# Chunked attention and a gated FFN in one kernel: sums and values in two PSUM tiles, memory keys by SyncE, constants laid early, another order in blocks 0 and 1

## The chip, the cores and the metric

The kernel runs on one core of a Trainium2 chip. TensorE (PE in the rows) multiplies matrices and writes to PSUM, ScalarE (ACT) and VectorE (DVE) read and write PSUM and SBUF, GpSimd (POOL) builds masks and issues the DMAs that convert from float32 to float16, and SyncE (SP) issues plain DMAs and DMA transposes. Each engine runs its own list of instructions in order and waits on semaphores. The metric is device microseconds of one execution, lower is better.

## The reference

Attention over chunks of 32 queries, each with 16 tokens of left context, 8 of right context and 8 memory tokens, then a feed-forward network without bias whose gate is a ReLU:

```python
batch, n_heads, seq, head_dim = (4, 8, 768, 64); n_mem = 8
for c in range(seq // 32):
    l_start, r_end = max(0, 32 * c - 16), min(S, 32 * c + 32 + 8)
    k_full = concatenate([mem_k, k[:, :, l_start:r_end]], axis=2)
    v_full = concatenate([mem_v, v[:, :, l_start:r_end]], axis=2)
    a = softmax(q_c @ k_full^T / sqrt(64))
    out[:, :, chunk] = a @ v_full
x = out.transpose(0, 2, 1, 3).reshape(3072, 512)
return (maximum(x @ w_gate, 0) * (x @ w_val)) @ w_out     # 512 -> 1536 -> 512
```

Inputs and output are float32; the kernel computes in float16 with float32 sums.

## The kernel before, in words

The 3072 tokens are cut into eight blocks of 384 (half a sequence). A block has four windows of 96 queries; a window sees 8 memory tokens and a band of up to 120 tokens, so that its scores are one matmul with 128 rows of keys. Heads go in pairs (`hp`, four of them), one head on each half of the partitions.

For a block `n` and a pair `hp` the steps are: `step_s` (in block 0 `step_s0`, which adds the mask by a matmul): the scores on TensorE and their exponential on ScalarE into `ex`; `step_d`: the sums of `ex` over the keys, by four matmuls with a matrix of ones into `xs`; `step_l`: ScalarE's logarithm of `xs`, in place (line 258); `step_e`: ScalarE's exponential of minus that, the reciprocal `rinv` (line 262); `step_v`: the values, eight matmuls into `xo` (line 269); `step_m`: VectorE's product of `xo` and `rinv` into `xT`, the input of the FFN. The tile `X` (`x_ps` in the rows) holds both, `xo` in its first bank of PSUM and `xs` in its second, and there is one such tile.

The FFN of a block is twelve units (`ffn_unit`, eight matmuls each: four with the gate's weights, four with the value's, into one of two PSUM buffers `f_ps`; then ScalarE's ReLU and VectorE's product) and three output units (`out_unit`, twelve matmuls each). Which block's attention step stands behind which unit is written out: by hand for blocks 0 and 1, by `run` for the others. `run` puts the sums, the logarithm and the values of a pair (`d`, `l`, `v`) in a row between the two halves of a unit, two units behind the pair's scores, the exponential behind that unit, and the product ahead of the next one.

Keys and queries of blocks 0 and 1 come as rows and are turned on TensorE (`turn_pe`, then `turn_copy` on VectorE); those of block 2 and later come as bands and are turned by DMA transposes that SyncE issues (`turn_dma`, lines 204 and 206). Half of block 0's rows are staged in float32 (`kst` by SyncE, `qst` by ScalarE's queue) and cast; everything else comes by POOL, in the order of its list, whose numbers are the program's. `fill` issues matmuls on a tile of zeros whose result nobody reads. The framework adds a wait wherever two instructions touch the same tile region in conflicting ways, so far as it can tell them apart.

Of the kernel before, what the change touches and what calls it, by code (L numbers as in the profile page):

```python
# [8 lines left out]
F32 = mybir.dt.float32  # L9
# [8 lines left out]
def kernel(  # L18
# [28 lines left out]
    J = 4  # L47
# [30 lines left out]

    ident = const.tile([128, 128], F16, name="ident")
    sels = [const.tile([128, NQ, 32], F16, name=f"sel{p}") for p in range(2)]  # L80
    kst = const.tile([KR, H // 2, J * D], F32, name="kst")
    qst = const.tile([QR, H // 2, J * D], F32, name="qst")
    k16s = [const.tile([128, NQ, H, D], F16, name=f"k16{p}") for p in range(2)]
    vwins = [const.tile([128, NQ, H, D], F16, name=f"vwin{p}") for p in range(2)]
# [3 lines left out]
    maskk = const.tile([128, 128], F16, name="maskk")  # L88
    maskq = const.tile([128, QB], F16, name="maskq")
    filler = const.tile([128, 512], F16, name="filler")  # L90
    X = xps.tile([128, 2, 512], F32, name="x_ps")
    xo, xs = X[:, 0, 0:TB], X[:, 1, 0:TB]
    mln64 = const.tile([128, 1], F32, name="mln64")
    wg = const.tile([128, NFC, DFF], F16, name="wg")
    wv = const.tile([128, NFC, DFF], F16, name="wv")
# [24 lines left out]
    def load_rows_mem(n):  # L120
        src = bass.AP(tensor=mem_k.tensor, offset=mem_k[n // 2, 0, 0, 0].offset,
                      ap=[[J * D, 2], [NMEM * D, H], [1, J * D]])
        pool_dma(rows_of(n)[0][KR:KR + 2], src)
# [125 lines left out]
    def step_d(n, hp):  # L249
        ex = exs[n, hp]  # L250
        parts = [(0, 1, 1), (1, NQ, 0)] if n % 2 == 0 else [(0, NQ - 1, 0), (NQ - 1, NQ, 2)]
        for i0, i1, kind in parts:
            for hh in range(2):
                nc.tensor.matmul(xs[D * hh:D * hh + D, QB * i0:QB * i1], lhsT=ones[:, kind, :],  # L254
                                 rhs=ex[:, hh, i0:i1, :], start=True, stop=True)

    def step_l(n, hp):
        nc.scalar.activation(xs, xs, ACT.Ln, scale=1.0 / 64.0)  # L258

    def step_e(n, hp):  # L260
        rinv = rpool.tile([128, TB], F32, name="rinv")
        nc.scalar.activation(rinv, xs, ACT.Exp, scale=-1.0, bias=mln64)  # L262
        rinvs[n, hp] = rinv
# [58 lines left out]
            out_unit(n, u - NDC, between)  # L322


    def fill(count, cols=512):
        ps = fps.tile([128, 2, 512], F32, tag="f", name="idle")
        for i in range(count):
            nc.tensor.matmul(ps[:, 0, 0:cols], lhsT=filler[:, 0:128], rhs=filler[:, 0:cols], start=True, stop=True)


    nc.scalar.preload_act_table_set("natural_log_exp_and_others")
    for hp in range(HP // 2):
        sp(kst[:, 2 * hp:2 * hp + 2], k_rows(0, 2 * hp, 2))
        act_dma(qst[:, 2 * hp:2 * hp + 2], q_rows(0, 2 * hp, 2))
    load_rows_mem(0)
    fetch_mem(memv, mem_v)

    def words(t):
        return t.bitcast(U32)

    zero(filler, 0.0)
    zero(words(ident), 0)
    zero(words(sels[0].rearrange("p i t -> p (i t)")), 0)


    zero(words(maskk), 0)
    zero(words(maskq), 0)
# [11 lines left out]
    zero(ones[96:128, 2], 0.0)  # L359
    zero(ones[96:120, 2], 1.0)  # L360
    zero(mln64, -LN64)
    zero(words(vwins[0][0:NMEM + 16, 0].rearrange("p h d -> p (h d)")), 0)
    zero(words(vwins[1][96:128, NQ - 1].rearrange("p h d -> p (h d)")), 0)

    def select(ap, fill_with, base, pattern, mult, op=ALU.not_equal):
        nc.gpsimd.affine_select(out=ap, in_=ap, compare_op=op, fill=fill_with, base=base, pattern=pattern,
# [10 lines left out]

    select(ident, 1.0, 0, [[-1, 128]], 1)
    build_sel(0)
    load_rows(0, 4, 4)  # L380
    loads_v(0)
    load_w(0, 256)
    load_w(256, 512)

    def cast(t, hp, eng):
        dst, src = rows_of(0)[t], (kst, qst)[t]
        eng(dst[0:(KR, QR)[t], 2 * hp:2 * hp + 2], src[:, 2 * hp:2 * hp + 2])

    fill(9)
    cast(0, 0, dve_copy)  # L390
    cast(1, 0, act_copy)
    turn_pe(0, 0)
    turn_copy(0, 0)
    fill(3)
    cast(0, 1, act_copy)
    cast(1, 1, act_copy)
    step_s0(0, 0)
    turn_pe(0, 1)
    turn_copy(0, 1)
    fill(1)  # L400
# [12 lines left out]
    step_v(0, 0)
    step_m(0, 0)
    step_s0(0, 3)
    step_d(0, 2)
    step_l(0, 2)
    step_e(0, 2)


    zero(words(sels[1].rearrange("p i t -> p (i t)")), 0)
    build_sel(1)
    zero(bias, 0.0)
    zero(words(k16s[0][0:32, 0].rearrange("p h d -> p (h d)")), 0)
    zero(words(k16s[1][96:128, NQ - 1].rearrange("p h d -> p (h d)")), 0)
    load_w(512, 1024)
    load_rows_mem(1)
    load_rows(1, 0, 4)
    load_rows(1, 4, 4)

    select(bias, NEG, -NMEM, [[-32, 3]], 1, ALU.is_ge)
    select(bias, 0.0, -NMEM, [[0, 3]], 1, ALU.is_ge)
    select(bias, NEG, NMEM + 55, [[32, 3]], -1, ALU.is_ge)
    load_w(1024, 1280)
    loads_v(1)
    load_w(1280, 1536)
# [44 lines left out]
    step_s(1, 2)
    step_d(1, 0)
    step_l(1, 0)
    step_e(1, 0)
    step_v(1, 0)
    step_m(1, 0)
    ffn_unit(0, 9)
    step_s(1, 3)
    step_d(1, 1)
    step_l(1, 1)  # L490
    step_e(1, 1)
    step_v(1, 1)
    step_m(1, 1)
    ffn_unit(0, 10)
    step_d(1, 2)
    step_l(1, 2)
    step_e(1, 2)
    step_v(1, 2)
    step_m(1, 2)
    ffn_unit(0, 11)  # L500
    step_d(1, 3)
    step_l(1, 3)
    step_e(1, 3)
    step_v(1, 3)
    step_m(1, 3)
# [68 lines left out]
```

## Time and profile before

| | before |
|---|---|
| median of 3 runs | 275.13 us (273.32 to 278.44) |
| the profiled execution | 276.26 us, span 274.6 us |
| mean granted clock of TensorE | 0.975 |
| TensorE busy | 242.1 us, 88% of the span |
| ScalarE busy | 128.5 us, 47% |
| VectorE busy | 81.1 us, 30% |
| POOL busy | 87.7 us, 32% |

The span runs from the first to the last instruction of the profiled execution; the time around it is 1.7 us. A busy share is an average over the whole span, which has stages with different limits. The granted clock is the share of TensorE's full clock that was granted: 1.00 is 2.4 GHz and 0.50 is 1.2 GHz; values between are stretches with both.

### The profile page before, as it was taken

Reading aid. Unit: us, or ns where it says so; the run is one execution under the profiler, and the core shown is the slowest. Engines: PE = TensorE matmul, PEld = TensorE weight load, DVE = VectorE, ACT = ScalarE, POOL = GpSimd, SP = SyncE. Lnnn points to the kernel's source line nnn. Section 1 sums busy time; section 2 is a strip of 40 time slices with the busy share of each in tenths; the row PEclk is TensorE's granted clock in tenths of the full one; section 3 lists DMA queues with packets and bytes.
Section 4 is the critical chain, followed back from the end, with each engine's and each line's share of the span. In section 5 each row is a group of like instructions: output and inputs, shape, how many; then the busy total and the mean of one; then the engine's idle time right before and its main releaser. Section 6 shows DMA issues by size and latency. Waiting matters only on the chain.

```text
span 274.6 us, 4565 instructions
## 1 busy us (share of the span) xinstructions
PE 242.1 (88%) x1845; PEld 128.9 (47%) x1845; DVE 81.1 (30%) x161; ACT 128.5 (47%) x276; POOL 87.7 (32%) x116
## 2 busy tenths in 40 slices
PE   5957983889998999999899999899999998999994
PEld 1633562445444455544454455444554454545541
DVE  3533472223033124321334033311342033313420
ACT  4442347232475256634565266534664365623421
POOL 8757789236901930077003910050000000000000
PEclk9988999669999999999999999999999999999999
DMA  7999999999993998199931996094600200011002
GB/s 153 162 138 198 180 166 181 172 145 157 174 180 91 133 183 117 24 58 187 144 72 11 153 160 134 2 94 111 127 0 2 115 0 4 0 76 41 0 29 85
DMA packets 113780, 28.56 MB, mean 104 GB/s; under 512 B 100224, under 2 KB 110688, under 8 KB 113760
## 3 DMA queue, kind: packets, MB, share of 16 engines
q0 software_dynamic: 86960, 15.17, 69.0%
q1 hardware_dynamic: 26384, 12.72, 19.8%
q10 hardware_dynamic: 416, 0.39, 0.5%
q8 instruction: 14, 0.23, 0.4%
q14 instruction: 6, 0.05, 0.1%
HBM read 31.15 MB, written 6.29 MB: 136 GB/s over the span
## 4 chain that ended last, share of the span: by engine, by line
PE 85%; ACT 9%; DMA 2%; issue 1%; DVE 1%; DVEq 0%; ACTq 0%; POOLq 0%
PE f_ps L286 49%; PE o_ps L311 23%; ACT x_ps L258 5%; PE x_ps L269 4%; PE x_ps L254 3%; PE sc_ps L218 3%; DMA rk<-in_mem_k_dram 2%; ACT rinv L262 1%; ACT ex L240 1%; PE kq_ps L185 1%; PE kq_ps L190 1%; ACT gr L292 1%; DVE gv L293 0%; DVE kq L199 0%; PE sc_ps L226 0%
## 5 line engine op out<-in xcount | busy, mean ns | idle before, releaser
L293 DVE TENSOR_TENSOR gv<-f_ps,gr 128x384 f16<-128x384 f32 x96 | 53.4, 557 | 151.6 <-ACT gr L292 151.6
L286 PE MATMUL f_ps<-xT,wg 128*128 128x384 f16 x384 | 81.5, 333 | 0.8 <-DVE gv L293 0.8
L286 PE MATMUL f_ps<-xT,wv 128*128 128x384 f16 x384 | 81.6, 333 | 0.0
L292 ACT ACTIVATE gr<-f_ps 128x384 f16<-128x384 f32 x96 | 47.0, 491 | 71.4 <-PE f_ps L286 69.4
L311 PE MATMUL o_ps<-wo,gv 128*128 128x512 f16 x288 | 63.8, 379 | 0.0
L136 POOL DMA_DIRECT2D vwin<-in_v_dram x32 | 28.8, 910 | 75.0 <-PE x_ps L269 72.2
L286 PEld LDWEIGHTS <-wg 128*128 128x128 f16 x384 | 35.6, 99 | 26.5 <-issue 2.4
L286 PEld LDWEIGHTS <-wv 128*128 128x128 f16 x384 | 36.2, 99 | 24.4 <-issue 1.9
L311 PEld LDWEIGHTS <-gv 128*128 128x128 f16 x288 | 28.0, 98 | 32.8
L314 ACT COPY o_sb<-o_ps 128x512 f32<-128x512 f32 x24 | 14.0, 585 | 45.2 <-PE o_ps L311 45.2
L240 ACT ACTIVATE ex<-sc_ps,bias 128x256 f16<-128x256 f32 x84 | 33.5, 477 | 2.5 <-PE sc_ps L218 2.5
L269 PE MATMUL x_ps<-ex,vwin 128*64 128x96 f16 x256 | 12.1, 215 | 24.3 <-ACT x_ps L258 13.6
L269 PEld LDWEIGHTS <-vwin 128*64 128x64 f16 x256 | 11.0, 113 | 29.4 <-issue 29.0
L273 DVE TENSOR_TENSOR xT<-x_ps,rinv 128x384 f16<-128x384 f32 x32 | 17.8, 555 | 23.3 <-PE x_ps L269 13.8
L136 POOL DMA_DIRECT2D k<-in_k_dram x24 | 21.5, 911 | 6.5 <-DMA wo<-in_moe_w_out_dram 5.5
L258 ACT ACTIVATE x_ps<-x_ps 128x384 f32<-128x384 f32 x32 | 15.3, 478 | 15.6 <-PE x_ps L254 15.5
L157 POOL DMA_DIRECT2D q16n<-in_q_dram x24 | 18.7, 807 | 6.2 <-DMA vwin<-in_v_dram 4.9
L262 ACT ACTIVATE rinv<-x_ps,mln 128x384 f32<-128x384 f32 x32 | 18.4, 576 | 0.2
L254 PE MATMUL x_ps<-ex,ones 128*64 128x96 f16 (+1 forms) x128 | 11.7, 264 | 0.0
L199 DVE CAST kq<-kq_ps 128x896 f16<-128x896 f32 x8 | 8.7, 1090 | 5.8 <-PE kq_ps L190 5.8
L254 PEld LDWEIGHTS <-ones 128*64 128x64 f16 x128 | 4.8, 110 | 10.1 <-issue 9.9
L218 PEld LDWEIGHTS <-kT 64*128 64x128 f16 x192 | 4.8, 94 | 7.8 <-issue 7.8
(51 smaller groups left out, 67.6 us busy)
## 6 DMA issues: line engine op xcount, KB each, us to landing
out_dram<-o_sb SPq DMA_DIRECT2D x24, 256.0 KB, 2.3
vwin<-in_v_dram POOLq DMA_DIRECT2D x24, 120.0 KB, 4.9
q16n<-in_q_dram POOLq DMA_DIRECT2D x24, 96.0 KB, 6.4
k<-in_k_dram POOLq DMA_DIRECT2D x18, 120.0 KB, 6.3
wo<-in_moe_w_out_dram POOLq DMA_DIRECT2D x3, 512.0 KB, 9.7
wg<-in_moe_w_gate_dram POOLq DMA_DIRECT2D x4, 256.0 KB, 7.8
wv<-in_moe_w_val_dram POOLq DMA_DIRECT2D x4, 256.0 KB, 8.0
rk<-in_k_dram POOLq DMA_DIRECT2D x3, 224.0 KB, 7.4
```

The costliest lines, as they stand in the source:

```text
L136: pool_dma(dsts[p][NMEM + m0:NMEM + m1, i], src)
L157: pool_dma(q16s[n][:, i], src)
L240: nc.scalar.activation(ex[:, :, :, s], src, ACT.Exp, scale=SCALE, bias=bias[:, g:g + 1])
L254: nc.tensor.matmul(xs[D * hh:D * hh + D, QB * i0:QB * i1], lhsT=ones[:, kind, :], rhs=ex[:, hh, i0:i1, :], start=True, stop=True)
L258: nc.scalar.activation(xs, xs, ACT.Ln, scale=1.0 / 64.0)
L262: nc.scalar.activation(rinv, xs, ACT.Exp, scale=-1.0, bias=mln64)
L269: nc.tensor.matmul(xo[D * hh:D * hh + D, QB * i:QB * i + QB], lhsT=vw[:, i, 2 * hp + hh, :], rhs=ex[:, hh, i, :], start=True, stop=True)
L273: nc.vector.tensor_tensor(out=x_of(n)[:, hp, :], in0=xo, in1=rinvs.pop((n, hp)), op=ALU.mult)
L286: nc.tensor.matmul(ps[:, a, 0:TB], lhsT=(wg, wv)[a][:, f, 128 * m:128 * m + 128], rhs=xTs[n][:, f, :], start=(f == 0), stop=(f == NFC - 1))
L292: nc.scalar.activation(gr, ps[:, 0, 0:TB], ACT.Relu)
L293: nc.vector.tensor_tensor(out=gvs[n][:, m, :], in0=ps[:, 1, 0:TB], in1=gr, op=ALU.mult)
L311: nc.tensor.matmul(o_ps, lhsT=gvs[n][:, m, 128 * t:128 * t + 128], rhs=wo[:, m, :], start=(m == 0), stop=(m == NDC - 1))
```

## The change

Sums and values get two tiles of one bank each, so that `xo` and `xs` are tiles of their own. The memory keys of heads 0 to 3 of block 0 go by SyncE, between its two loads of staged keys, into two further rows of `kst`, and are cast with them; both casts of keys are now on VectorE and both of queries on ScalarE. POOL loads the rows of heads 4 to 7 first. The memsets of `sel1`, `bias` and the window of block 0's values stand ahead of the attention of block 0; those of the other windows come after it. The weights are loaded in the order 0, 256, 512 (256 columns each), then block 1's rows, then 768, block 1's values, and 1024 to 1536 in one piece. The fillers are 18 matmuls of 384 columns into `xo` instead of 13 of 512 into a buffer of the FFN. In block 0 the order of turns, scores and sums is another; in block 1 the turns stand two units earlier, and the sums of a pair stand a unit ahead of its values.

```diff
-    kst = const.tile([KR, H // 2, J * D], F32, name="kst")
+    kst = const.tile([KR + 2, H // 2, J * D], F32, name="kst")
...
-    X = xps.tile([128, 2, 512], F32, name="x_ps")
-    xo, xs = X[:, 0, 0:TB], X[:, 1, 0:TB]
+    xo, xs = (xps.tile([128, 512], F32, name=nm)[:, 0:TB] for nm in ("xo_ps", "xs_ps"))
...
-        sp(kst[:, 2 * hp:2 * hp + 2], k_rows(0, 2 * hp, 2))
+        sp(kst[0:KR, 2 * hp:2 * hp + 2], k_rows(0, 2 * hp, 2))
         act_dma(qst[:, 2 * hp:2 * hp + 2], q_rows(0, 2 * hp, 2))
-    load_rows_mem(0)
-    fetch_mem(memv, mem_v)
+        if hp == 0:
+            load_rows_mem(sp, kst[KR:KR + 2], 0, 0, H // 2)
+    load_rows(0, 4, 4)
+    load_rows_mem(pool_dma, rows_of(0)[0][KR:KR + 2, H // 2:H], 0, H // 2, H // 2)
...
+    zero(words(sels[1].rearrange("p i t -> p (i t)")), 0)
+    zero(bias, 0.0)
...
-    load_rows(0, 4, 4)
+    fetch_mem(memv, mem_v)
     loads_v(0)
-    load_w(0, 256)
-    load_w(256, 512)
+    for c0 in (0, 256, 512):
+        load_w(c0, c0 + 256)
...
-    fill(9)
-    cast(0, 0, dve_copy)
-    cast(1, 0, act_copy)
-    turn_pe(0, 0)
-    turn_copy(0, 0)
-    fill(3)
-    cast(0, 1, act_copy)
-    cast(1, 1, act_copy)
+    fill(11)
+    for hp in range(2):
+        cast(0, hp, dve_copy)
+        cast(1, hp, act_copy)
+        turn_pe(0, hp)
+        turn_copy(0, hp)
+    fill(4)
     step_s0(0, 0)
...
-    load_w(512, 1024)
-    load_rows_mem(1)
+    load_rows_mem(pool_dma, rows_of(1)[0][KR:KR + 2], 1, 0, H)
     load_rows(1, 0, 4)
     load_rows(1, 4, 4)
...
-    load_w(1024, 1280)
+    load_w(768, 1024)
+    zero(words(vwins[1][96:128, NQ - 1].rearrange("p h d -> p (h d)")), 0)
     loads_v(1)
-    load_w(1280, 1536)
+    load_w(1024, 1536)
...
-    for m in range(2, 8):
+    for m in range(2, 6):
         ffn_unit(0, m)
     turn_pe(1, 0)
     turn_copy(1, 0)
...
+    ffn_unit(0, 6)
+    sums(1, 0)
+    step_s(1, 2)
+    ffn_unit(0, 7)
+    sums(1, 1)
+    step_s(1, 3)
+    values(1, 0)
     ffn_unit(0, 8)
```

Here `sums` is `d`, `l`, `e` of a pair and `values` is `v`, `m`.

TensorE in block 3, where the second pair's sums and values stand between the halves of a unit (`ones` are the sums, `vwin` the values; the numbers in brackets name the semaphore of the engine that is waited for). Before:

```order
L254 MATMUL x_ps<-ex,ones 64x288 [waits Activation_49]
L254 LDWEIGHTS ones
L254 MATMUL x_ps<-ex,ones 64x288
L254 LDWEIGHTS ones
L254 MATMUL x_ps<-ex,ones 64x96
L254 LDWEIGHTS ones
L254 MATMUL x_ps<-ex,ones 64x96
L269 LDWEIGHTS vwin_101
L269 MATMUL x_ps<-ex,vwin_101 64x96 [waits Activation_49]
```

And now:

```order
L253 MATMUL xs_ps<-ex,ones 64x288 [waits Activation_49]
L253 LDWEIGHTS ones
L253 MATMUL xs_ps<-ex,ones 64x288
L253 LDWEIGHTS ones
L253 MATMUL xs_ps<-ex,ones 64x96
L253 LDWEIGHTS ones
L253 MATMUL xs_ps<-ex,ones 64x96
L268 LDWEIGHTS vwin_101
L268 MATMUL xo_ps<-ex,vwin_101 64x96
```

Nothing moved here; the first matmul of the values no longer names ScalarE's semaphore.

POOL at the start of the program, from the end of block 0's values on (`sel_95` is block 1's selection matrix, `rk` and `rq` block 1's rows). Before:

```order
L170 DMA wv<-in_moe_w_val_dram 128x4x256
L366 AFFINE_SELECT sel_95<-sel_95 128x4x28
L366 AFFINE_SELECT sel_95<-sel_95 128x3x2
L366 AFFINE_SELECT sel_95<-sel_95 128x4x2
L170 DMA wg<-in_moe_w_gate_dram 128x4x512
L170 DMA wv<-in_moe_w_val_dram 128x4x512
L123 DMA rk<-in_mem_k_dram 2x8x256
```

And now:

```order
L169 DMA wg<-in_moe_w_gate_dram 128x4x256
L169 DMA wv<-in_moe_w_val_dram 128x4x256
L368 AFFINE_SELECT sel_95<-sel_95 128x4x28
L368 AFFINE_SELECT sel_95<-sel_95 128x3x2
L368 AFFINE_SELECT sel_95<-sel_95 128x4x2
L122 DMA rk<-in_mem_k_dram 2x8x256
```

The weights from column 512 on moved ahead of the selects, cut to 256 columns, and block 1's rows follow the selects at once; the other 256 columns come behind those rows.

ScalarE in block 1, where the attention stands between the units of block 0 (`gr` is the ReLU of a unit). Before, with the first pair's logarithm and exponential:

```order
L240 ACTIVATE ex<-sc_ps,bias 128x8x32 x6
L292 ACTIVATE gr<-f_ps 128x384
L240 ACTIVATE ex<-sc_ps,bias 128x8x32 x3
L258 ACTIVATE x_ps<-x_ps 128x384
L262 ACTIVATE rinv<-x_ps,mln_110 128x384
```

And now:

```order
L239 ACTIVATE ex<-sc_ps,bias 128x8x32 x6
L291 ACTIVATE gr<-f_ps 128x384
L257 ACTIVATE xs_ps<-xs_ps 128x384
L261 ACTIVATE rinv<-xs_ps,mln_111 128x384
L239 ACTIVATE ex<-sc_ps,bias 128x8x32 x3
```

The first pair's logarithm and exponential moved ahead of the third pair's three score exponentials.

## Rows read from the trace of the kernel before

**Rows 1.** the page's part 4: the chain that ended last, by line

```profile
PE f_ps L286 49%; PE o_ps L311 23%; ACT x_ps L258 5%; PE x_ps L269 4%; PE x_ps L254 3%; PE sc_ps L218 3%; DMA rk<-in_mem_k_dram 2%; ACT rinv L262 1%; ACT ex L240 1%; PE kq_ps L185 1%; PE kq_ps L190 1%; ACT gr L292 1%; DVE gv L293 0%; DVE kq L199 0%; PE sc_ps L226 0%
```

**Rows 2.** waits: engine, line, waited for: us in total, times, longest

```profile
PE x_ps L269 <- ACT x_ps L258: 13.6, 24, 0.6
PE x_ps L269 <- ACT rinv L262: 10.7, 7, 2.1
```

**Rows 3.** timeline of TensorE, one pair: start, us, [idle before <-releaser]

```profile
99.25 0.81 PE L286 MATMUL f_ps<-xT,wg 128*128 128x384 f16 x4
99.99 0.36 PE L254 MATMUL x_ps<-ex,ones 128*64 128x288 f16 x4
100.92 0.36 PE L269 MATMUL x_ps<-ex,vwin 128*64 128x96 f16 x8 [0.57 <-ACT x_ps L258]
101.21 0.82 PE L286 MATMUL f_ps<-xT,wv 128*128 128x384 f16 x4
```

**Rows 4.** timeline of TensorE, block 0: sums and what follows

```profile
10.38 0.36 PE L254 MATMUL x_ps<-ex,ones 128*64 128x96 f16 x4
10.57 0.60 PE L185 MATMUL kq_ps<-sel,rk 114*64 114x128 f16 x8
```

**Rows 5.** windows: us; busy us PE, PEld, DVE, ACT, POOL; clock, DMA share, GB/s

```profile
119.00:149.00 30.00, 27.73 (x213) 14.55 (x211) 8.57 (x16) 15.67 (x35) 10.07 (x13) 1.00 0.96 106
```

**Rows 6.** DMA issues around 1.2 to 2.1: KB each, us to landing

```profile
kst<-in_k_dram SPq DMA_DIRECT2D x2, 224.0 KB, 3.6
rk<-in_mem_k_dram POOLq DMA_DIRECT2D x1, 8.0 KB, 5.2
```

**Rows 7.** timeline of VectorE: the first copy of a turn

```profile
7.74 1.09 DVE L199 CAST kq<-kq_ps 128x896 f16<-128x896 f32 x1 [2.85 <-PE kq_ps L190]
```

**Rows 8.** timeline of TensorE, 0 to 72: four starts with their waits

```profile
6.75 0.63 PE L185 MATMUL kq_ps<-sel,rk 114*64 114x128 f16 x8 [1.52 <-DMA rk<-in_mem_k_dram]
43.56 0.36 PE L269 MATMUL x_ps<-ex,vwin 128*64 128x96 f16 x8 [2.10 <-ACT rinv L262]
56.44 0.53 PE L269 MATMUL x_ps<-ex,vwin 128*64 128x96 f16 x8 [1.19 <-ACT rinv L262]
68.80 0.34 PE L218 MATMUL sc_ps<-qT,kT 64*128 64x96 f16 x8
```

**Rows 9.** windows, columns as in 5: two stretches with a low granted clock

```profile
18.75:22.95 4.20, 3.70 (x27) 1.39 (x21) 1.11 (x2) 0.46 (x1) 4.06 (x9) 0.60 1.10 156
49.71:59.33 9.62, 7.25 (x41) 3.62 (x41) 2.23 (x4) 3.05 (x6) 2.53 (x3) 0.50 1.54 159
```

**Rows 10.** timeline of POOL: block 1's selects

```profile
16.73 0.62 POOL L366 TENSOR_SCALAR_AFFINE_SELECT sel<-sel 128x112 f16<-128x112 f16 x3 [4.95 <-DVE bias L423]
```

**Rows 11.** windows of 1 us: the last two numbers are DMA share and GB/s

```profile
18.00:19.00 1.00, 0.48 (x9) 0.35 (x9) 0.00 (x0) 0.47 (x1) 1.00 (x3) 0.85 0.46 23
19.00:20.00 1.00, 1.00 (x4) 0.30 (x2) 0.56 (x1) 0.00 (x0) 1.00 (x2) 0.50 0.66 59
20.00:21.00 1.00, 1.00 (x11) 0.48 (x11) 0.19 (x1) 0.00 (x0) 1.00 (x3) 0.50 1.20 197
```

**Rows 12.** timeline of SyncE's queue: staged keys, block 2's transposes

```profile
0.81 0.90 SPq L333 DMA_DIRECT2D kst<-in_k_dram  x2
44.39 7.42 SPq L204 DMA_TRANSPOSE kT<-k  x1
51.99 4.74 SPq L206 DMA_TRANSPOSE qT<-q16n  x1
```

**Rows 13.** DMA issues at 44.39, 51.99, and 76.9 to 82.5: transposes, us to landing

```profile
kT<-k SPq DMA_TRANSPOSE x1, 14.2
...
qT<-q16n SPq DMA_TRANSPOSE x1, 11.3
...
kT<-k SPq DMA_TRANSPOSE x1, 6.9
qT<-q16n SPq DMA_TRANSPOSE x1, 3.7
```

More of the change, by code (lines that the diff above doesn't have):

```diff
@@ L118, in rows_of, with load_rows_mem @@
         return rows[n]
[L120 to L123, printed above, removed]
+    def load_rows_mem(dma, dst, n, h0, nh):
+        src = bass.AP(tensor=mem_k.tensor, offset=mem_k[n // 2, h0, 0, 0].offset,
+                      ap=[[J * D, 2], [NMEM * D, nh], [1, J * D]])
+        dma(dst, src)
     def load_rows(n, h0, nh):
@@ L322, in unit, with fill @@
             out_unit(n, u - NDC, between)
-    def fill(count, cols=512):
-        ps = fps.tile([128, 2, 512], F32, tag="f", name="idle")
+    def fill(count, cols=TB):
         for i in range(count):
-            nc.tensor.matmul(ps[:, 0, 0:cols], lhsT=filler[:, 0:128], rhs=filler[:, 0:cols], start=True, stop=True)
+            nc.tensor.matmul(xo[:, 0:cols], lhsT=filler[:, 0:128], rhs=filler[:, 0:cols], start=True, stop=True)
     nc.scalar.preload_act_table_set("natural_log_exp_and_others")
     for hp in range(HP // 2):
-        sp(kst[:, 2 * hp:2 * hp + 2], k_rows(0, 2 * hp, 2))
+        sp(kst[0:KR, 2 * hp:2 * hp + 2], k_rows(0, 2 * hp, 2))
         act_dma(qst[:, 2 * hp:2 * hp + 2], q_rows(0, 2 * hp, 2))
-    load_rows_mem(0)
-    fetch_mem(memv, mem_v)
+        if hp == 0:
+            load_rows_mem(sp, kst[KR:KR + 2], 0, 0, H // 2)
+    load_rows(0, 4, 4)
+    load_rows_mem(pool_dma, rows_of(0)[0][KR:KR + 2, H // 2:H], 0, H // 2, H // 2)
     def words(t):
         return t.bitcast(U32)
-    zero(filler, 0.0)
     zero(words(ident), 0)
     zero(words(sels[0].rearrange("p i t -> p (i t)")), 0)
+    zero(words(filler), 0)
+    zero(words(vwins[0][0:NMEM + 16, 0].rearrange("p h d -> p (h d)")), 0)
     zero(words(maskk), 0)
@@ L361 @@
     zero(mln64, -LN64)
-    zero(words(vwins[0][0:NMEM + 16, 0].rearrange("p h d -> p (h d)")), 0)
-    zero(words(vwins[1][96:128, NQ - 1].rearrange("p h d -> p (h d)")), 0)
+    zero(words(sels[1].rearrange("p i t -> p (i t)")), 0)
+    zero(bias, 0.0)
     def select(ap, fill_with, base, pattern, mult, op=ALU.not_equal):
@@ L379 @@
     build_sel(0)
-    load_rows(0, 4, 4)
+    fetch_mem(memv, mem_v)
     loads_v(0)
-    load_w(0, 256)
-    load_w(256, 512)
+    for c0 in (0, 256, 512):
+        load_w(c0, c0 + 256)
     def cast(t, hp, eng):
-        dst, src = rows_of(0)[t], (kst, qst)[t]
-        eng(dst[0:(KR, QR)[t], 2 * hp:2 * hp + 2], src[:, 2 * hp:2 * hp + 2])
-    fill(9)
-    cast(0, 0, dve_copy)
-    cast(1, 0, act_copy)
-    turn_pe(0, 0)
-    turn_copy(0, 0)
-    fill(3)
-    cast(0, 1, act_copy)
-    cast(1, 1, act_copy)
+        dst, src, n = rows_of(0)[t], (kst, qst)[t], (KR + 2, QR)[t]
+        eng(dst[0:n, 2 * hp:2 * hp + 2], src[:, 2 * hp:2 * hp + 2])
+    fill(11)
[5 more added lines that the diff above has]
+    fill(4)
     step_s0(0, 0)
-    turn_pe(0, 1)
-    turn_copy(0, 1)
-    fill(1)
+    turn_pe(0, 2)
+    turn_copy(0, 2)
     step_d(0, 0)
     step_l(0, 0)
+    step_s0(0, 1)
     step_e(0, 0)
-    turn_pe(0, 2)
-    step_s0(0, 1)
-    turn_copy(0, 2)
     turn_pe(0, 3)
+    turn_copy(0, 3)
+    fill(1)
+    step_s0(0, 2)
     step_d(0, 1)
     step_l(0, 1)
-    step_s0(0, 2)
-    turn_copy(0, 3)
     step_e(0, 1)
+    fill(2)
+    step_s0(0, 3)
     step_v(0, 0)
     step_m(0, 0)
-    step_s0(0, 3)
     step_d(0, 2)
@@ L418 @@
     step_e(0, 2)
-    zero(words(sels[1].rearrange("p i t -> p (i t)")), 0)
     build_sel(1)
-    zero(bias, 0.0)
-    zero(words(k16s[0][0:32, 0].rearrange("p h d -> p (h d)")), 0)
-    zero(words(k16s[1][96:128, NQ - 1].rearrange("p h d -> p (h d)")), 0)
-    load_w(512, 1024)
-    load_rows_mem(1)
+    load_rows_mem(pool_dma, rows_of(1)[0][KR:KR + 2], 1, 0, H)
     load_rows(1, 0, 4)
@@ L433 @@
     select(bias, NEG, NMEM + 55, [[32, 3]], -1, ALU.is_ge)
-    load_w(1024, 1280)
+    load_w(768, 1024)
+    zero(words(vwins[1][96:128, NQ - 1].rearrange("p h d -> p (h d)")), 0)
     loads_v(1)
-    load_w(1280, 1536)
+    load_w(1024, 1536)
+    zero(words(k16s[0][0:32, 0].rearrange("p h d -> p (h d)")), 0)
+    zero(words(k16s[1][96:128, NQ - 1].rearrange("p h d -> p (h d)")), 0)
     fetch_mem(memk, mem_k)
@@ L454 @@
     chunk(0, 0)
+    step_d(0, 3)
+    step_l(0, 3)
+    step_e(0, 3)
     step_v(0, 2)
@@ L457 @@
     chunk(0, 1)
-    step_d(0, 3)
-    step_l(0, 3)
-    step_e(0, 3)
     step_v(0, 3)
@@ L466, with sums, values @@
     loads_v(2)
-    for m in range(2, 8):
+    def sums(n, hp):
+        step_d(n, hp)
+        step_l(n, hp)
+        step_e(n, hp)
+    def values(n, hp):
+        step_v(n, hp)
+        step_m(n, hp)
+    for m in range(2, 6):
         ffn_unit(0, m)
@@ L479 @@
     turn_copy(1, 3)
-    ffn_unit(0, 8)
[L481 to L486, printed above, removed]
-    ffn_unit(0, 9)
[L488 to L493, printed above, removed]
-    ffn_unit(0, 10)
[L495 to L499, printed above, removed]
-    ffn_unit(0, 11)
[L501 to L505, printed above, removed]
+    ffn_unit(0, 6)
[5 more added lines that the diff above has]
+    values(1, 0)
+    ffn_unit(0, 8)
+    values(1, 1)
+    sums(1, 2)
+    ffn_unit(0, 9)
+    values(1, 2)
+    sums(1, 3)
+    ffn_unit(0, 10)
+    values(1, 3)
+    ffn_unit(0, 11)
     STEP = {"s": step_s, "d": step_d, "l": step_l, "e": step_e, "v": step_v, "m": step_m}
```

## The prediction

> **What bounds the kernel now.** I read the chain that ended last first, by line: TensorE's FFN and output matmuls hold 72% of it, but ScalarE's logarithm, line 258, is third with 5% [rows 1]. A function that should run beside TensorE has no business there. The list of waits says whom it holds up: the value matmuls of line 269 waited 24 times for line 258, 13.6 us in all, and 7 times for the exponential of line 262, 10.7 us [rows 2]. The first turn, at 6.75, waited 1.52 us for the memory keys [rows 8]. 24 is six blocks times four head pairs, so the first wait is the steady part, and the timeline shows one: sums at 99.99, values only at 100.92, with 0.57 us idle between, though the values read nothing that the logarithm writes [rows 3]. The seven others lie in blocks 0 and 1, ahead of the first scores of block 2 at 68.80 [rows 8]. So I cost two stretches apart: from 68.80 to the end, where TensorE alone sets the pace, and from 0 to 68.80, where transfers may.
>
> **The steady part: two tiles.** The sums and the values of a pair lay in one PSUM tile, so each value group waited for line 258 to have done with that tile. In the changed program no first value matmul waits for ScalarE any more; some wait for VectorE's multiplication of the pair before, one to three units earlier. What is saved for a pair is 0.93 us from the start of the sums to the start of the values [rows 3], less what the sums take when something follows at once. That is bounded by 0.19 us (sums at 10.38, next group at 10.57 [rows 4]) and by 0.29 us, the time of the value group, which has as many columns and twice the weight loads [rows 3]. That leaves 0.64 to 0.74; the idle time alone would give 0.57. I take 0.65, near the lower end, since weights change shape there: 24 x 0.65 = **15.6 us** (13.7 to 17.8). What is late next? ScalarE has 15.67 us of work in 30 us, VectorE 8.57 [rows 5]; with TensorE some 2.6 us faster per block ScalarE stands at 57%, and the logarithm now runs under the values and the second half of the unit, so I add nothing.
>
> **The start.** The keys of memory for heads 0 to 3 now go by SyncE into the staging tile. They took 5.2 us from POOL's issue, the staged keys 3.6 us from SyncE's [rows 6]. SyncE starts at 0.81 and needs 0.45 us an issue [rows 12]; issued second they land near 0.81 + 0.45 + 3.6 = 4.9. With half a microsecond for the cast, now of 114 rows, the first turn starts at 5.4 for 6.75: 1.3 us earlier. The second half of the staged keys is issued one place later, about 0.45 us, which nobody waits for: its cast stands behind a copy of 1.09 us on VectorE [rows 7]. That queueing is the price of taking the cast from ScalarE: the second turn comes about 1 us later than it might. The fillers are 18 x 384 columns for 13 x 512, 4% more, into the values' tile, which is free then: nothing.
>
> **Blocks 0 and 1.** In block 1 the sums of a pair are now issued a unit ahead of its values, so that the logarithm and the exponential run under an FFN unit (twice four matmuls of 0.7 us [rows 3]). Its four waits, two of 2.10 (43.56) and two of 1.19 (56.44) [rows 8], 6.6 us, go. Of the other 4.1 us of the seven waits, in block 0, I take 3, since there two of the waits are replaced by waits for the same ScalarE queue. With the waits went the clock: the granted clock was 0.60 over 18.75 to 22.95 and 0.50 (1.2 GHz of the two levels) over 49.71 to 59.33, the second time soon after the two waits of 2.10 us. TensorE was busy 3.70 and 7.25 us there [rows 9]; at 2.4 GHz these would be 2.2 and 3.6, so 1.5 + 3.6 = 5.1 are to be had. If only TensorE counted, the scores of block 2 would come 1.3 - 1.0 + 3 + 6.6 + 5.1 = 15.0 us earlier, at 53.8.
>
> **But the transfers do not move by 15 us.** Those scores need the transposes of block 2's keys and queries, which SyncE issued at 44.39 and 51.99 [rows 12] and which landed 14.2 and 11.3 us later [rows 13], at 58.6 and 63.3: 5.5 us ahead of their use at 68.80. They follow the loads of block 2, which are at the end of POOL's list, behind all weights, keys and values of blocks 0 and 1, and the changed list carries the same bytes ahead of them. The engines that move them were busy all the while but for one hole: POOL waited 4.95 us for a memset [rows 10], and the rate fell to 23 and 59 GB/s in two microseconds beside 197 [rows 11]. The constants laid early take this wait away: (2 x 197 - 82) / 197 = 1.6 us. Block 0's rows now ahead of POOL's selects fill up to another 1 us between 5 and 9, where POOL's issue was the limit; I take 0.5. So the queries land at 63.3 - 2.1 = 61.2 and the scores move by **7.6 us** (5.5 if the loads do not move at all, 15.0 if the transposes cease to matter). TensorE stands idle for the rest, 61.2 - 53.8 = 7.4 us, at the first scores of block 2. Splitting weights 512 to 1023 in two and joining 1024 to 1535 moves no bytes; unit 8 may wait up to 1 us for the joined load, inside those 7.4.
>
> What the skill says to this: the Trainium skill, DMA: Bandwidth & Descriptors (Issuing engines are not separate DMA queues), has all issuers run on the same 16 engines, so that issuing elsewhere saves the issue time alone. The rates of rows 11 agree; taken strictly it would give the move to SyncE nothing beyond its 1.3 us, which the idle time swallows.
>
> **After that idle time the clock is low.** The two stretches of rows 9 cost 1.5 and 3.6 us, the second behind idle times of 2.10 us. A 7 us gap is longer, but the output unit behind it is dense, like the units that ended both; I take **2 us** (0 to 3.6). The Trainium skill, TensorE: Matmul & The Clock Gate (HAM oscillation), describes the same: a wait for data sends the array to half its clock, and the next work starts cold. No stretch of this trace has a gap of that length, so only the direction is borne out.
>
> **The sum**, against the profiled execution's 276.26 us: 15.6 + 7.6 - 2.0 = 21.2, so 255.1. That execution lies 0.4% above the median of 275.13; from the median, 253.9: I say **254**.
>
> **Rivals.**
> 1. The transposes do not hold TensorE. For it: later transposes landed in 6.9 and 3.7 us, half and a third of 14.2 and 11.3 [rows 13]; if block 2's meet a shorter queue to that degree, the queries are there by about 51.99 - 2.1 + 3.7 = 53.6. Against: the weights of the output, the next values and keys are queued beside them as before. Then 275.1 - 15.6 - 15.0 = 244.5. Chance 0.20.
> 2. The first part gives nothing: the loads come no earlier, and the cold stretch after the wait eats the 5.5 us of slack. Against it: rows 11 show a hole that a memset made. Then 275.1 - 13.7 = 261.4. Chance 0.10.
> 3. The wait in the steady part stays under another name: the values then wait for VectorE's multiplication, or the next unit for ScalarE. Against: that multiplication is issued a unit or more ahead, and ScalarE has 43% to spare. Only the first part is left: 275.1 - 5.6 = 269.5. Chance 0.05.
> 4. Slower: the clock stays at 1.2 GHz after TensorE's wait for the transposes, because block 2's scores, sums and values interrupt the units of that stretch. Every microsecond of work there costs a second one. It decides from 23 us of such work, and is worth 281 from 29 us. Against: the longest such stretch had 3.6 us of work (7.25 at half), and in all steady blocks, with a wait in every third unit, the clock was 1.00 [rows 5]. Chance 0.02.
>
> **How the numbers follow.** Forecast 0.60 (249 to 260: 17.8 + 7.6 at one end, 13.7 + 5.5 - 3.6 at the other), rivals 0.20, 0.10, 0.05, 0.02, other things 0.03. The range 244 to 261 holds the forecast's case, most of the first rival's and some of the second's: 0.8. About 2% is what can be told from no change; 269.6 is that bound. Faster 0.95, within 2% 0.03, slower 0.02.
>
> **What the changed profile would show.** Right: no wait of the values for the logarithm; each steady block 2.6 us shorter from its first scores to the next block's; the four waits of block 1 gone; the last wait of TensorE ahead of block 2's first scores 4 to 8 us long, put down to a transfer; clock 0.5 for a few microseconds behind it and 1.00 ahead of it. The prediction is wrong if those scores come before 57 or after 65, if steady blocks keep a wait above 0.2 us, or if the low clock behind the transposes lasts longer than 8 us.

## The result and the profile after

| | before | after |
|---|---|---|
| median | 275.72 us (4 runs, 273.32 to 278.44) | 251.79 us (4 runs, 251.0 to 254.03) |
| the profiled execution | 276.26 us, span 274.6 | 251.0 us, span 249.3 |
| mean granted clock | 0.975 | 0.983 |
| TensorE busy | 242.1 us, 88% | 235.5 us, 94% |

The ratio is 0.917, with a 95% interval of 0.908 to 0.927. The forecast of 254 us and its range hold the time. Here and below medians are over all runs, while ratios leave out executions more than 1.5% above the fastest of the same kernel.

The chain by line, which had line 258 in third place [rows 1]:

```profile
PE f_ps L285 43%; PE o_ps L310 25%; DMA wv<-in_moe_w_val_dram 8%; DMA qT<-q16n 4%; DMA wo<-in_moe_w_out_dram 3%; PE xs_ps L253 3%; PE sc_ps L217 3%; POOL vwin L135 3%; PE xo_ps L268 2%; SPq L203 1%; POOL wg L169 1%; POOL wv L169 1%; POOL q16n L156 1%; POOL rk L126 0%; POOL memv L138 0%
```

No line of ScalarE is left. In its place stand loads: weights, the queries' transpose and POOL's issues. The chain leaves TensorE and goes back through loads, so that one wait for data decides what lies ahead of it. The list of TensorE's waits names it in its first line, and neither line of [rows 2] has a successor:

```profile
PE sc_ps L217 <- DMA qT<-q16n: 4.0, 1, 4.0
PE kq_ps L184 <- DVE rk L389: 1.7, 1, 1.7
...
PE xo_ps L268 <- DVE xT L272: 0.7, 2, 0.4
```

A steady pair in TensorE's timeline, beside [rows 3]: the values start 0.19 us behind the sums, where 0.93 us lay between, and nothing is idle.

```profile
89.92 0.36 PE L253 MATMUL xs_ps<-ex,ones 128*64 128x288 f16 x4
90.11 0.34 PE L268 MATMUL xo_ps<-ex,vwin 128*64 128x96 f16 x8
90.38 0.82 PE L285 MATMUL f_ps<-xT,wv 128*128 128x384 f16 x4
```

That is 0.74 us a pair, 24 x 0.74 = 17.8 us. The first 67 us in the same view: the first two turns, the first output unit, and the first scores of block 2, which [rows 8] had at 68.80 with no wait.

```profile
5.21 0.74 PE L184 MATMUL kq_ps<-sel,rk 114*64 114x128 f16 x8
...
7.96 0.63 PE L184 MATMUL kq_ps<-sel,rk 114*64 114x128 f16 x8 [1.68 <-DVE rk L389]
...
53.42 2.75 PE L310 MATMUL o_ps<-wo,gv 128*128 128x512 f16 x12
60.20 0.51 PE L217 MATMUL sc_ps<-qT,kT 64*128 64x96 f16 x8 [4.03 <-DMA qT<-q16n]
60.64 5.46 PE L310 MATMUL o_ps<-wo,gv 128*128 128x512 f16 x18
66.03 0.36 PE L253 MATMUL xs_ps<-ex,ones 128*64 128x96 f16 x4
```

Windows, with the columns of [rows 5]; the third number from the end is the granted clock. It is low in two stretches, one behind the wait of 1.68 us and one behind that of 4.03 us; the two of [rows 9] are gone.

```profile
9.00:12.40 3.40, 3.40 (x28) 1.99 (x28) 1.05 (x1) 0.81 (x1) 3.40 (x6) 0.51 1.92 154
...
60.00:61.00 1.00, 0.80 (x9) 0.46 (x10) 0.00 (x0) 0.26 (x1) 0.66 (x2) 0.55 2.13 181
61.00:62.00 1.00, 1.00 (x4) 0.41 (x3) 0.00 (x0) 0.94 (x3) 0.48 (x1) 0.50 1.64 260
62.00:63.00 1.00, 1.00 (x4) 0.35 (x3) 0.00 (x0) 0.00 (x0) 0.22 (x1) 0.50 2.22 176
63.00:64.00 1.00, 1.00 (x5) 0.35 (x4) 0.00 (x0) 0.00 (x0) 1.00 (x2) 0.74 2.41 153
```

SyncE's queue issued block 2's transposes 2.4 and 3.0 us earlier than in [rows 12], and the keys' landed 13.2 us later (14.2 in [rows 13]):

```profile
42.04 6.74 SPq L203 DMA_TRANSPOSE kT<-k  x1
48.97 4.56 SPq L205 DMA_TRANSPOSE qT<-q16n  x1
```

So of the 25.3 us between the two profiled executions, 8.6 came ahead of the first scores of block 2 (68.80 to 60.20). The stretch behind them fell from 205.8 to 189.1 us, by 16.7, which is the pairs' 17.8 less the low clock.

### The profile page after: what moved, and what is told of

It reads as the page before. It is cut to its first block, busy times and chain, and to the rows that moved or that the text cites. A ratio compares the mean times of both kernels' runs of the same rounds, so it can differ in the third digit from the quotient of the medians.

```text
span 249.3 us, 4594 instructions
## 1 busy us (share of the span) xinstructions
PE 235.5 (94%) x1850; PEld 127.1 (51%) x1850; DVE 81.3 (33%) x162; ACT 127.6 (51%) x275; POOL 87.4 (35%) x116
## 4 chain that ended last, share of the span: by engine, by line
PE 74%; DMA 15%; POOL 6%; issue 2%; SPq 1%; ACT 0%; POOLq 0%
PE f_ps L285 43%; PE o_ps L310 25%; DMA wv<-in_moe_w_val_dram 8%; DMA qT<-q16n 4%; DMA wo<-in_moe_w_out_dram 3%; PE xs_ps L253 3%; PE sc_ps L217 3%; POOL vwin L135 3%; PE xo_ps L268 2%; SPq L203 1%; POOL wg L169 1%; POOL wv L169 1%; POOL q16n L156 1%; POOL rk L126 0%; POOL memv L138 0%
## 5 line engine op out<-in xcount | busy, mean ns | idle before, releaser
L285 PE MATMUL f_ps<-xT,wg 128*128 128x384 f16 x384 | 79.4, 327 | 0.8 <-DVE gv L292 0.8
L285 PE MATMUL f_ps<-xT,wv 128*128 128x384 f16 x384 | 79.3, 327 | 0.0
L310 PE MATMUL o_ps<-wo,gv 128*128 128x512 f16 x288 | 65.2, 385 | 0.0
L272 DVE TENSOR_TENSOR xT<-xo_ps,rinv 128x384 f16<-128x384 f32 x32 | 17.7, 553 | 17.3 <-ACT rinv L261 14.4
L257 ACT ACTIVATE xs_ps<-xs_ps 128x384 f32<-128x384 f32 x32 | 15.3, 479 | 11.8 <-PE xs_ps L253 10.2
L261 ACT ACTIVATE rinv<-xs_ps,mln 128x384 f32<-128x384 f32 x32 | 18.4, 576 | 0.2
L217 PE MATMUL sc_ps<-qT,kT 64*128 64x96 f16 x192 | 8.4, 208 | 4.0 <-DMA qT<-q16n 4.0
L268 PE MATMUL xo_ps<-ex,vwin 128*64 128x96 f16 x256 | 11.0, 207 | 0.7 <-DVE xT L272 0.7
L253 PE MATMUL xs_ps<-ex,ones 128*64 128x96 f16 (+1 forms) x128 | 11.4, 258 | 0.0
L268 PEld LDWEIGHTS <-vwin 128*64 128x64 f16 x256 | 8.7, 110 | 2.8 <-issue 2.4
```

Of the source, the lines that this page charges most:

```text
L217: nc.tensor.matmul(sc[:, hh, QB * i:QB * i + QB], lhsT=kT[s, i, hp, :], rhs=qT[s, i, hp, :], start=start, stop=start or i == NQ - 1)
L268: nc.tensor.matmul(xo[D * hh:D * hh + D, QB * i:QB * i + QB], lhsT=vw[:, i, 2 * hp + hh, :], rhs=ex[:, hh, i, :], start=True, stop=True)
L272: nc.vector.tensor_tensor(out=x_of(n)[:, hp, :], in0=xo, in1=rinvs.pop((n, hp)), op=ALU.mult)
L285: nc.tensor.matmul(ps[:, a, 0:TB], lhsT=(wg, wv)[a][:, f, 128 * m:128 * m + 128], rhs=xTs[n][:, f, :], start=(f == 0), stop=(f == NFC - 1))
L310: nc.tensor.matmul(o_ps, lhsT=gvs[n][:, m, 128 * t:128 * t + 128], rhs=wo[:, m, :], start=(m == 0), stop=(m == NDC - 1))
```

## The experiments

The theory is the prediction's: two tiles give the steady part, and in the first 60 us the transposes hold what the other edits free. The rivals were that the edits other than the tiles carry the first part, or that the transposes do not matter. Unless said otherwise an edit is made to the changed kernel.

**The two tiles alone**, in the kernel before:

```diff
-    X = xps.tile([128, 2, 512], F32, name="x_ps")
-    xo, xs = X[:, 0, 0:TB], X[:, 1, 0:TB]
+    xo, xs = (xps.tile([128, 512], F32, name=nm)[:, 0:TB] for nm in ("xo_ps", "xs_ps"))
```

> The kernel before with the two tiles alone. Theory (the shared tile costs 0.74 us a pair in the steady part, and the first scores of block 2 cannot start before their queries are turned): 24 x 0.74 = 17.8 less behind those scores; in blocks 0 and 1 the values no longer wait for ScalarE either, so TensorE comes to the scores early and waits there for the queries at about 63.3 instead of 68.8, 5.5 less, and some 1.6 us are lost to the low clock behind that wait: 275.7 - 17.8 - 5.5 + 1.6 = 254. Rival (the new order of blocks 0 and 1 and the early loads carry the first part): the scores stay near 68.8, 275.7 - 17.8 = 258.

Measured: 253.93 us (253.15 to 254.28), ratio 0.925 (0.920 to 0.930). Two lines of one edit bring 21 of the 23 us or so. In TensorE's timeline the output unit is done by 58.0 and the scores wait from there:

```profile
55.27 2.75 PE L310 MATMUL o_ps<-wo,gv 128*128 128x512 f16 x12
62.71 0.35 PE L217 MATMUL sc_ps<-qT,kT 64*128 64x96 f16 x8 [4.69 <-DMA qT<-q16n]
```

This kernel has the order of before in blocks 0 and 1, and yet no value group in it waits for the exponential. So those seven waits of [rows 2], 10.7 us, came from the shared tile too: the values read `ex`, and `rinv` is needed by VectorE's product only. What came in their place is a smaller wait of two FFN units for that product, which the changed kernel with its new order does not have:

```profile
PE f_ps L285 <- DVE xT L272: 1.9, 2, 1.1
```

**One tile, all other edits kept**: the three lines above turned round.

> The changed kernel with sums and values back in one tile. Theory: the 24 waits come back, 17.8 us, and the first scores of block 2 still start near 60 to 62, since TensorE had 4 us in hand there: 251.8 + 17.8 = 269.6, up to 272. Rival (the steady gain came from the other parts, for instance a ScalarE that is no longer late): it stays near 252.

Measured: 275.26 us (10 runs, 274.66 to 276.52), ratio 1.003 (1.000 to 1.006). Neither number was met; the loss is larger than my theory said. Its waits:

```profile
PE x_ps L269 <- ACT x_ps L258: 13.6, 24, 0.6
PE x_ps L254 <- DVE xT L273: 3.4, 3, 1.3
PE x_ps L269 <- ACT rinv L262: 3.4, 3, 1.2
...
PE x_ps L327 <- ACT rinv L262: 2.1, 2, 1.6
```

The 24 waits are back to the tenth. The other three lines lie in blocks 0 and 1: sums that now follow each other wait for the product of the pair before, and even the fillers, which write `xo`, wait for ScalarE. The clock went with them, 0.50 over 10 us and 6.92 us of work:

```profile
20.00:30.00 10.00, 6.92 (x53) 3.23 (x48) 3.05 (x7) 2.76 (x5) 7.51 (x10) 0.50 1.74 182
```

At full clock that work takes 3.5 us. Without the tiles the other edits give no gain.

**The first scores of block 2 two output units later**, so that 5.3 us of output matmuls run while the transposes land:

```diff
     run([(1, m) for m in range(6)] + [(0, NDC + t) for t in range(NT)] + [(1, m) for m in range(6, NDC + NT)],
-        2, 6, 2, 2, 9)
+        2, 8, 2, 2, 9)
```

> The changed kernel with block 2's scores two units later in the list (behind the third output unit instead of the first), nothing else. Theory: the wait for the queries, 4.0 us, and the low clock behind it, 1.6 us, both go, since 5 us of output matmuls now stand ahead of the scores: 251.8 - 5.6 = 246.2. Rival (the transfers are late as a whole, so the wait only moves to block 2's values or to block 3's transposes, or the shorter distance to the end of the block brings a new one): 250 to 252.

Measured: 246.93 us (245.67 to 247.12), ratio 0.899 (0.895 to 0.903). TensorE goes from the output units to the scores without a wait, and the granted clock is 1.00 over 50 to 70:

```profile
55.18 7.93 PE L310 MATMUL o_ps<-wo,gv 128*128 128x512 f16 x36
63.05 0.34 PE L217 MATMUL sc_ps<-qT,kT 64*128 64x96 f16 x8
```

The wait was on the path, then, and cost 4.9 us with what the clock took.

**The same in the kernel before with two tiles**, which leaves out every other edit:

```diff
-        2, 6, 2, 2, 9)
+        2, 8, 2, 2, 9)
```

> The kernel before with the two tiles and with block 2's scores two units later, so without any of the new orders, loads and constants. It asks what these are worth once the wait for the queries is out of the way. Theory (they bring TensorE to the end of block 1 some 2 us earlier, 55.9 against 58.0, and only the wait hid this): 246.9 + 2 = 249, with no wait at the first scores. Rival (they are worth nothing, or the loads without them come too late for the later scores): 247, or 252 and more with the wait back.

Measured: 247.76 us (247.06 to 248.43), ratio 0.900 (0.896 to 0.904), between the two expectations. The later issue of its transposes shows as a rest of the wait:

```profile
64.04 0.34 PE L217 MATMUL sc_ps<-qT,kT 64*128 64x96 f16 x8 [1.03 <-DMA qT<-q16n]
```

With the wait covered, loads, constants and order are worth 247.76 - 246.93 = 0.8 us together, against the 2.1 us (253.93 - 251.79) with the wait uncovered. These are medians of different sets of runs, and the intervals of the ratios overlap in both pairs, so only their smallness is shown. The two profiles show no gain ahead of the wait either: the output units start at 55.08 here and at 55.18 in the kernel with all edits, whose first matmuls ran at half speed (see the last section).

**What the low clock costs**: 20 matmuls of zeros, whose result nobody reads, ahead of the scores that wait.

```diff
                 pieces(n, [("e", hp) for hp in now])
+                if n == 2 and u == first:
+                    fill(20)
                 pieces(n, [("s", hp) for hp in range(HP) if u == s_at[hp]])
```

> The changed kernel with 20 matmuls on zeros (3.3 us of work) ahead of block 2's first scores, so that TensorE is busy during most of its wait for the queries. They add no result. Theory (the low clock behind the wait costs 1.6 us by itself): the scores start when they did, and the output units behind them run at full clock: 251.8 - 1.6 = 250.2. Rival (the low clock was not due to the idle time): 251.8, with the granted clock at 0.5 behind the scores as before.

Measured: 252.48 us (249.7 to 254.39), ratio 0.917 (0.909 to 0.924). The median cannot tell the two apart; the timeline can:

```profile
56.91 3.41 PE L326 MATMUL xo_ps<-filler 128*128 128x384 f16 x20
62.70 0.35 PE L217 MATMUL sc_ps<-qT,kT 64*128 64x96 f16 x8 [2.38 <-DMA qT<-q16n]
62.98 4.06 PE L310 MATMUL o_ps<-wo,gv 128*128 128x512 f16 x18
66.97 0.36 PE L253 MATMUL xs_ps<-ex,ones 128*64 128x96 f16 x4
```

The 18 output matmuls behind the scores took 66.97 - 62.98 = 3.99 us at clock 1.00, and 66.03 - 60.64 = 5.39 in the changed kernel. So 1.4 us is the price of the low clock in that execution. It is not a fixed price: the same 18 matmuls took 5.68 us behind the wait with the tiles alone, and 6.51 and 6.58 us in two kernels below, which is 1.7 to 2.6 us more than at full clock. The gain was lost in this execution because the queries landed at 62.70, not 60.20: with nothing changed ahead of it, that landing moves by 2.5 us.

**The two memsets late**, as before the change:

```diff
-    zero(words(sels[1].rearrange("p i t -> p (i t)")), 0)
-    zero(bias, 0.0)
...
+    zero(words(sels[1].rearrange("p i t -> p (i t)")), 0)
+    zero(bias, 0.0)
     build_sel(1)
```

> The changed kernel with the memsets of block 1's selection matrix and of the bias back behind the attention of block 0, as before. Theory (the transfers run without a hole and set when the queries of block 2 are turned): POOL waits some 5 us, a hole of 1.6 to 2 us comes back into the transfers, the first scores of block 2 move from 60.2 to about 62, and the time from 251.8 to 253.5. Rival (POOL's wait is covered by what is queued): no hole, scores at 60.2, 251.8.

Measured: 253.92 us (253.35 to 256.17), ratio 0.925 (0.920 to 0.931). POOL waits again, where the changed kernel has its selects at 12.98 without a wait, and the rest follows: the first transpose is issued at 43.12 for 42.04, the scores start at 61.57 for 60.20.

```profile
16.81 0.62 POOL L366 TENSOR_SCALAR_AFFINE_SELECT sel<-sel 128x112 f16<-128x112 f16 x3 [3.73 <-DVE bias L420]
```

By the medians that is 2.1 us for two memsets whose results TensorE needs only much later (the intervals of the ratios overlap), and not all of it is the loads:

```profile
52.28 2.75 PE L310 MATMUL o_ps<-wo,gv 128*128 128x512 f16 x12
61.57 0.51 PE L217 MATMUL sc_ps<-qT,kT 64*128 64x96 f16 x8 [6.54 <-DMA qT<-q16n]
62.01 6.58 PE L310 MATMUL o_ps<-wo,gv 128*128 128x512 f16 x18
68.52 0.36 PE L253 MATMUL xs_ps<-ex,ones 128*64 128x96 f16 x4
```

TensorE came to the output units 1.1 us earlier than in the changed kernel and waited the longer. The scores moved by 1.4 us, and the output matmuls behind them took 1.1 us more at the low clock (6.51 for 5.39); together that is the 2.5 us between the two profiled executions (253.52 and 251.0). The rate of the transfers fell to 126 GB/s at the lowest, in the microsecond from 20 to 21, and not to the 23 of [rows 11]: most of POOL's wait was covered by what was queued.

**Why the transposes take so long.** In the changed kernel the loads of block 2's values and of block 3 wait until TensorE has passed the third unit of block 1:

```diff
-    loads_v(2)
...
+            if n == 2 and u == 2:
+                nc.tensor.matmul(xo[:, 0:64], lhsT=filler[:, 0:128], rhs=hold, start=True, stop=True)
+                select(hold, 0.0, 0, [[-1, 64]], 1)
+                loads_v(2)
+                loads(3)
...
-    loads(3)
```

> The changed kernel with POOL held, by one small matmul that its next instruction waits for, until TensorE is through the third unit of block 1 (about 49.5): the loads of block 2's values and all of block 3 are issued then instead of from 41.2 on. It asks why the transposes of block 2 take 13 and 11 us. Theory (they share the transfer engines with what POOL queues beside them): with only the output's weights beside them they land some 5 us earlier, the wait of 4.0 us and the low clock behind it go, 251.8 - 5.6 = 246.2. Rival (they take that long by themselves or by SyncE's issue): the scores still start at 60 to 62, 251.8; or the values of block 2 are now late, 252 and more.

Measured: 250.59, 250.99, 246.19 and 250.83 us. The transpose of the keys landed in 11.2 us for 13.2, and the scores started 1.65 us earlier, at the end of a shorter wait:

```profile
58.55 0.51 PE L218 MATMUL sc_ps<-qT,kT 64*128 64x96 f16 x8 [3.52 <-DMA qT<-q16n]
```

Neither expectation fits three of the runs, and one comes out at 246.2; that one has no profile, so why is not known. In the profiled execution, of 250.59 us, 1.2 of the 1.65 us went back to the low clock behind the wait, where the 18 output matmuls took 6.58 us (58.98 to 65.56) for 5.39:

```profile
58.98 6.64 PE L311 MATMUL o_ps<-wo,gv 128*128 128x512 f16 x18
65.56 0.36 PE L254 MATMUL xs_ps<-ex,ones 128*64 128x96 f16 x4
```

The edit did not thin what moves beside the transposes: the DMA engines moved 200 GB/s from 42 to 49 and 168 from 49 to 58, where the changed kernel has 199 and 158. So it does not answer its question, and whether sharing is what makes the transposes long stays open.

**Both pairs of casts ahead of the first copy**, since the second turn waits 1.68 us for a cast that stands behind the copy on VectorE; with the scores two output units later:

```diff
     for hp in range(2):
         cast(0, hp, dve_copy)
         cast(1, hp, act_copy)
+    for hp in range(2):
         turn_pe(0, hp)
         turn_copy(0, hp)
```

> The changed kernel with block 2's scores two units later, and with the casts of the second half of the staged rows ahead of the first copy on VectorE. Theory (the second turn waited 1.7 us for that cast, and the low clock from 9 to 12.4 us followed that wait): the second turn comes 1 us or more earlier, the low clock goes, 1.5 us, and with no wait at block 2's scores the whole shows: 246.9 - 2.5 = 244.4. Rival (the start is hidden behind ScalarE or behind the loads of block 1's rows): 246.9; or the staged rows land later than the first copy ends and the copy now waits: 247.5.

Measured: 245.23 us (244.89 to 247.27), ratio 0.892 (0.887 to 0.897), and once more, beside the next kernel:

> The kernel with both pairs of casts first once more, beside the one with the memory keys by POOL: 245.2 again under either theory; the difference of the two is what the memory keys by SyncE are worth.

Measured: 246.27 us (6 runs, 245.35 to 247.93), ratio 0.896 (0.890 to 0.902). Both are below the changed kernel's interval. Against 246.93 of the one without this edit the gain is not resolved by the medians, but the second run's timeline shows what it does:

```profile
7.05 0.63 PE L184 MATMUL kq_ps<-sel,rk 114*64 114x128 f16 x8 [0.89 <-DVE rk L389]
...
51.14 7.93 PE L310 MATMUL o_ps<-wo,gv 128*128 128x512 f16 x36
60.76 0.35 PE L217 MATMUL sc_ps<-qT,kT 64*128 64x96 f16 x8 [1.68 <-DMA qT<-q16n]
```

The second turn is 0.9 us earlier than in the changed kernel and the output units 2.3 us (53.42 to 51.14), and then 1.7 us of that goes into the wait for the queries. Not all of the 2.3 us is the edit's. In the profile of the first run the second turn came at 7.07 without a wait, and yet the matmuls ran at half speed until about 10.7 (four fillers in 1.46 us), and the output units started at 52.86:

```profile
8.70 1.46 PE L326 MATMUL xo_ps<-filler 128*128 128x384 f16 x4
```

So the expectation that the low clock goes with the wait is not borne out.

**Memory keys by POOL** as before the change, in that kernel:

```diff
-        if hp == 0:
-            load_rows_mem(sp, kst[KR:KR + 2], 0, 0, H // 2)
+    load_rows_mem(pool_dma, rows_of(0)[0][KR:KR + 2], 0, 0, H)
     load_rows(0, 4, 4)
-    load_rows_mem(pool_dma, rows_of(0)[0][KR:KR + 2, H // 2:H], 0, H // 2, H // 2)
```

> The kernel with both pairs of casts first, but the memory keys of all heads of block 0 by POOL again, as in the kernel before. Theory: TensorE sets the pace from the first turn to the end there, so the first turn at 6.7 for 5.2 (before: 6.75, waiting for the memory keys) moves everything by 1.3 to 1.5 us: 246.6. Rival: the queries of block 2 or the rows of heads 4 to 7 set the pace of the first 60 us, and the first turn's 1.5 us are swallowed by a later wait: 245.2, as without the edit.

Measured: 247.01 us (6 runs, 245.56 to 247.86), ratio 0.897 (0.892 to 0.903): 0.7 us more than its neighbour, which the spread of either does not resolve.

```profile
6.70 0.63 PE L184 MATMUL kq_ps<-sel,rk 114*64 114x128 f16 x8 [1.59 <-DMA rk<-in_mem_k_dram]
...
7.42 0.67 PE L184 MATMUL kq_ps<-sel,rk 114*64 114x128 f16 x8
```

The first turn is 1.5 us later, the second only 0.4 us (7.42 for 7.05), since the second cast is ready by then. My theory counted the first turn and should have counted the second: the rows give 0.4 us, and what there is of it can still vanish in the wait for the queries, 2.67 us in this execution. The Trainium skill, DMA: Bandwidth & Descriptors (Issuing engines are not separate DMA queues), holds that another issuer saves the issue alone. At the first turn these rows do not agree, and the measurement decides: the turn moved by 1.5 us, where POOL's issue of the keys took 0.71 us in this kernel; the keys landed 5.1 us behind it. Nor do [rows 11] bear on that rule, with which the prediction calls them in agreement: they show the rate falling while POOL waits, not two issuers side by side.

## Why the prediction was right, step by step

- **Steady part, 15.6 us: mechanism right, size short.** It was 17.8 us. I took 0.65 of a pair's 0.93 us since weights change shape there; the pair gave all of the upper bound, 0.74. The 0.19 us of [rows 4] was the row to go by. Nothing else became late: no steady value group waits for VectorE, and the next block's scores come 27.15 us behind (87.59 to 114.74), 3.0 us less than before (97.66 to 127.84).
- **The wait for the transposes: right, which was the main choice.** Scores at 60.20 for a forecast of 61.2; the wait 4.0 us for 7.4, since TensorE came at 56.2 and not at 53.8. The second turn cost 1.68 us where I had put about 1, and 3.4 us of work behind it ran at clock 0.51, which I had not foreseen (my signs had 1.00 ahead of the wait for the transposes): together 2.4 us more. In one profile with the casts first, neither is as large, and TensorE starts its output units at 51.14 and would be through with the first, which takes 2.75, at 53.9; in the other the low clock stayed without the wait. None of it counted, as the transposes held the scores anyway. That they landed within 1 us of the forecast is in part luck: in the kernel with zeros, with nothing changed ahead, the scores started at 62.70.
- **The low clock behind that wait, 2 us: it was 1.4** in the changed kernel, as the matmuls of zeros showed, and 1.7 to 2.6 in three others. The Trainium skill, TensorE: Matmul & The Clock Gate (HAM oscillation), describes such a wait; this trace bears it out with 0.55 and 0.50 in the three microseconds behind 4.0 us of idle time.
- **Where a step was wrong though its number held:** I gave the four waits of block 1 to the new order of sums and values. They were the shared tile's: with two tiles alone they are gone, and with the new order alone three waits of 1.0 to 1.2 us stay, and sums and fillers wait as well. My chain of reasons read "the values wait for the exponential" and did not ask whether the values read it, as I had asked of the logarithm.
- **POOL's wait for the memset: right.** I put 1.6 us on it. Undoing it moves the first scores by 1.4 us and the median by 2.1, with the wait for the queries uncovered; the rest is the low clock. The memory keys by SyncE were costed at 1.3 us and are worth 0.4 at the second turn, none at the end so far as the runs resolve.
- **The sum** was 15.6 + 7.6 - 2.0 = 21.2; measured terms are 17.8 + 8.6 - 1.4 = 25.0 of the 25.3 us between the two profiled executions. Rivals 2 to 4 fell: the low clock lasted some 3.5 us, and no steady wait came back. Rival 1 was not what happened, but its time of 244.5 is about what one gets by covering the transposes, with the casts first (245.2 and 246.3).

Open: why the queries land at 58.6 to 62.7 in kernels that issue them within 1.5 us of each other, what the transposes spend 11 us on, and what sets the clock in the first 14 us.

## What to carry to other kernels

When an engine waits for another, ask whether the waiting instruction reads or overwrites what the other one writes; if it does neither, a tile shared by two quantities makes the wait, and it makes it wherever the pattern stands, in hand-ordered code too. Cost such a fix stage by stage: it is worth its full time where TensorE sets the pace, and nothing where a transfer ends last, until other work is laid over that transfer. And of two loads, cost the one whose consumer comes last: an earlier first turn is worth nothing if the second sets the pace.

## What was unexpected in the hardware

The transpose of block 2's queries, issued at 48.97 in the changed kernel, at 49.68 in the one with zeros and at 49.22 in the one with held loads, was used at 60.20, 62.70 and 58.55: the later issue does not by itself give the later landing, and the DMA engines moved 158, 151 and 168 GB/s from 49 to 58.

At the start the granted clock in the profile is not the whole story. In the kernel with the scores two output units later the windows read 1.00 from 0 to 9 and from 9 to 13.7, yet its matmuls run at half speed until about 13.7: the four fillers ahead of the first scores take 1.46 us, as at clock 0.51 in the changed kernel, and 0.82 where the clock is full. In the kernel with the memory keys by POOL they do take 0.82. First a window and the timeline of TensorE of the former, then the timeline of the latter:

```profile
9.00:13.70 4.70, 4.70 (x38) 2.98 (x38) 1.09 (x1) 0.63 (x1) 4.70 (x10) 1.00 1.76 162
...
8.86 1.06 PE L184 MATMUL kq_ps<-sel,rk 114*64 114x128 f16 x8 [1.86 <-DVE rk L389]
...
10.49 1.46 PE L326 MATMUL xo_ps<-filler 128*128 128x384 f16 x4
```

```profile
8.36 0.82 PE L326 MATMUL xo_ps<-filler 128*128 128x384 f16 x4
```

In these runs the duration of equal matmuls tells the clock at the start more surely than the record of it. Nor does the wait of the second turn decide that clock: with the memsets late and with the loads held TensorE waited 1.52 us there and went on at full speed (0.82 us for the four fillers), while in the changed kernel, behind 1.68 us, they took 1.45.
